# Signs of layer 1's weights copied by VectorE instead of ScalarE, w_out's fold and subtraction moved, and new ranks for the planner

## The chip, the cores and the metric

The kernel runs on one core of a Trainium2 chip. The metric is the device time of one execution in microseconds (us); the lower the better. TensorE (PE) multiplies matrices, VectorE (DVE) and ScalarE (ACT) work elementwise, GpSimd (POOL) also, SyncE (SP) issues most of the DMAs.

## The reference

Attention of 4 batches, 8 heads, 576 positions and 64 channels (four heads with a local mask, four with a strided one), followed by two MLP layers over the 2304 tokens:

```
attn = softmax(mask(q k^T / 8)) v
x = attn as (2304, 512)
h = x @ w_in1;  g = max(0.01 h, h);            x = g @ w_out1      # layer 1, 512 -> 2048 -> 512
h = x @ w_in2;  g = relu(h) + log1p(exp(-|h|)); out = g @ w_out2   # layer 2, softplus
```

The four weights come as 64-bit words, 512 x 2048 or 2048 x 512 of them. Inputs are large enough that the products need more than f16.

## The kernel before, in words

**Products.** A factor is cut into two f16 parts, a high one and the rest, and a product is three matmuls (`mm3`: high by high, high by rest, rest by high; lines 462 to 464). Layer 1 goes by units of 288 tokens (u = 0 to 7): `plan_first` makes the hidden layer, called G0, G1, G2, ... here, `plan_second` the second product, S0, S1, S2, .... Layer 2 goes by 9 units of 256 tokens.

**Weights.** Each weight is prepared in four quarters of 128 x 2048 words. A quarter is loaded by one DMA into an area of the tiles `pair` (`load`); VectorE finds its largest value (`largest`, line 156), from which a power of two for scaling is made (`scale`); it shifts the low words (`low`, line 162). ScalarE scales the high words (`shift`, line 209). Between the two, the sign bit has to get into the low word: for the layer-1 weights W1 (w_in) and O1 (w_out) ScalarE does it behind `shift`, by writing the scaled value as f16 into the upper half of the low word (`sign_of_scaled`, line 205); for the layer-2 weights VectorE does it ahead of `shift`, by copying the sign bit as a 16-bit word (`sign`, line 198). Then VectorE joins the words (`merge`, line 214), ScalarE writes the high f16 part (`high`, line 221), and the rest is a subtraction: for W1 on GpSimd (`rest`, line 226), for O1 on VectorE together with a factor (`rest_of`, line 230). That factor `by` equalizes the scales of W1's quarters; before, `high` and `rest_of` both apply it to O1.

O1's four quarters share one scale (`plan_together`), so none can be scaled before all four are loaded and searched; a quarter of O1 is loaded into the area of W1's quarter of that number once that one has been cut. The high part of an odd quarter of O1 lies where the quarter before it was, and so waits for that one's rest.

**Order.** The program of every engine is written in the order that `Plan.run` finds while the kernel is built. It is a list scheduler: each step has an engine, a cost in us, its dependencies, the PSUM and SBUF places it takes and frees, and a rank. Among the steps that could start on an engine within 0.5 us of the earliest, the one with the lowest rank goes first. A step marked `port` and every step of GpSimd also share one "port" clock. A rank is a pair (start, slope) of the table `RANKS` by the step's name, start + slope x index. Names: L0 to L3 loads of the batches' q, k, v; LW1, LO1, LW2, LO2 loads of weights; A and B the attention's scores and what follows; W1r, W1m, O1r, O1m the steps of a weight before and from its scale; G0, G1, G2, S0, S1, S2 the layer-1 units so named; M later units; F, Fd, Fa, Fp, S layer 2 on PE, DVE, ACT, POOL and PE again. Up to 130 us of its own clock the planner fills longer gaps of PE with matmuls on an identity whose result nobody reads (`idle`, line 92); the profile counts them as busy.

In the schedule before, the attention of batch 0 and the first W1 quarter come first, then G0, G1 and G2 with the attention of batch 1 and the rest of W1 beside them, then O1 and S0, S1, S2, and the later units, with layer 2's weights prepared beside these. S0 takes O1 quarter by quarter; S1 wants all of it.

Of the kernel before, what the change touches and what calls it, by code (L numbers as in the profile page):

```python
# [10 lines left out]
F16 = mybir.dt.float16  # L11
F32 = mybir.dt.float32
# [3 lines left out]
AF = mybir.ActivationFunctionType  # L16
ALU = mybir.AluOpType
# [4 lines left out]
B, H, S, D = 4, 8, 576, 64  # L22
# [15 lines left out]
RING = 5  # L38

RANKS = {  # L40
# [10 lines left out]
}  # L51

F64_LOW = 2.0 ** -11 * 1.625
# [2 lines left out]
def build(tc, qt, kl, ks, v, wi1, wo1, wi2, wo2, mloc, mstr, out):  # L56
    nc = tc.nc
    with ExitStack() as ctx:
# [79 lines left out]
        flat = lambda y: y.rearrange("p a b -> p (a b)")  # L138


        class Weight:
# [57 lines left out]
                    out=w[:, :, :, 1], in0=w[:, :, :, 3], scalar1=0x8000, scalar2=None, op0=ALU.bitwise_and  # L199
                )  # L200

            def sign_of_scaled(self, q):

                w = self.t[q].bitcast(F16).rearrange("p s (n t) -> p s n t", t=4)
                nc.scalar.activation(w[:, :, :, 1], self.words(q)[1].bitcast(F32), AF.Copy)  # L205

            def shift(self, q, s):
                lo, hi = self.words(q)
                nc.scalar.activation(hi.bitcast(F32), hi.bitcast(F32), AF.Copy, scale=s)  # L209
# [7 lines left out]
                )  # L217
                self.f[q] = f.bitcast(F32)

            def high(self, q, hl, by=1.0):  # L220
                nc.scalar.activation(flat(hl[0]), self.f[q], AF.Copy, scale=by)  # L221
                self.hl[q] = hl

            def rest(self, q, eng):
                hi, lo = self.hl[q]
                eng.tensor_tensor(out=flat(lo), in0=self.f[q], in1=flat(hi), op=ALU.subtract)  # L226

            def rest_of(self, q, by):
                hi, lo = self.hl[q]
                nc.vector.scalar_tensor_tensor(  # L230
                    out=flat(lo), in0=self.f[q], scalar=by, in1=flat(hi), op0=ALU.mult, op1=ALU.subtract
                )

            def scale_all(self, g):
                s = self.scale(0, g)
# [351 lines left out]
        W1, O1, W2, O2 = Weight("i1", wi1), Weight("o1", wo1), Weight("i2", wi2), Weight("o2", wo2)  # L587
# [112 lines left out]
        def plan_together(W, name, after, parts, then, w1):  # L700

            st, loads, read, made = {}, [], [], []
            step = lambda eng, cost, fn, deps, k, **kw: plan.add(
                eng, cost, fn, deps, (name + ("r" if k < 3 else "m"), k), **kw
            )
            m = once(lambda: sml.tile([P, 4], F32, name="m4", tag="wm4"))
            for q in range(4):
                ld = plan.add("SP", 5.9, lambda q=q: W.load(q, area(q)), after[q], ("L" + name, q))
                big = step("DVE", 2.2, lambda q=q: W.largest(q, m()[:, q : q + 1]), [ld], q)
                low = step("DVE", 1.14, lambda q=q: W.low(q), [ld], q + 0.1, port=True)  # L710
                loads.append(big)
                read.append([big, low])

            def over():
                st["m"] = sml.tile([P, 1], F32, name="m", tag="wm")
                nc.vector.tensor_reduce(out=st["m"], in_=m(), axis=AX.X, op=ALU.max)

            def all_over():
                st["g"] = to_all(st["m"])

            def scale():
                st["s"] = W.scale_all(largest_of(st["g"]))
                then()

            t = step("DVE", 0.1, over, loads, 3.05)
            t = step("PE", 0.35, all_over, [t], 3.05, take=["pt"])
            t = scaled = step("DVE", 2.3, scale, [t] + w1, 3.06, free=[t])
            for q in range(4):
                y = step("ACT", 2.07, lambda q=q: W.shift(q, st["s"]), [t] + read[q], 4 + q)
                y = step("ACT", 1.9, lambda q=q: W.sign_of_scaled(q), [y], 4 + q)  # L730
                y = step("DVE", 2.2, lambda q=q: W.merge(q), [y], 4 + q, port=True)
                y = step("ACT", 1.85, lambda q=q: W.high(q, parts(q), O1.by[:, q : q + 1]), [y] + made[-1:] * (q % 2), 4 + q)
                made.append(
                    step("DVE", 2.3, lambda q=q: W.rest_of(q, O1.by[:, q : q + 1]), [y], 4 + q, port=True)
                )
            return made, scaled

        def plan_quarter(W, name, q, place, after, parts, after_read, then=None, eng="DVE"):

            st = {}  # L740
            kind = lambda k: name + ("" if then is None else "r" if k < 0.25 else "m")
            step = lambda eng, cost, fn, deps, k, **kw: plan.add(eng, cost, fn, deps, (kind(k), q + k), **kw)

            def big():
                st["m"] = sml.tile([P, 1], F32, name="m", tag="wm")
                W.largest(q, st["m"])

            def over():
                st["g"] = to_all(st["m"])

            def scale():
                st["s"] = W.scale(q, largest_of(st["g"]))
                if then:
                    then(q)

            ld = plan.add("SP", 5.9, lambda: W.load(q, area(place)), after, ("L" + name, q))
            x = step("DVE", 2.2, big, [ld], 0)
            y = step("PE", 0.35, over, [x], 0, take=["pt"])
            sc = step("DVE", 1.45 if then else 1.05, scale, [y], 0.3, free=[y])
            y = step("DVE", 1.14, lambda: W.low(q), [ld], 0.1, port=True)  # L760
            if not then:
                y = step("DVE", 2.35, lambda: W.sign(q), [y], 0.2, port=True)
            y = step("ACT", 2.07, lambda: W.shift(q, st["s"]), [sc, x, y], 0.3)
            if then:
                y = step("ACT", 1.9, lambda: W.sign_of_scaled(q), [y], 0.3)
            y = step("DVE", 2.2, lambda: W.merge(q), [y], 0.4, port=True)
            y = step("ACT", 1.85, lambda: W.high(q, parts(q)), [y] + after_read, 0.5)
            if eng == "Pool":
                return step("Pool", 4.1, lambda: W.rest(q, nc.gpsimd), [y], 0.6), sc
            return step("DVE", 2.3, lambda: W.rest(q, nc.vector), [y], 0.6, port=True), sc  # L770
# [127 lines left out]
        A, A1 = at[0], at[1]  # L898
# [35 lines left out]
        by = lambda n, k=0: lambda i: (n, i + k)  # L934
# [4 lines left out]
        s = {0: plan_second_by_f(0, g[0], o1, by("S0"), a0 + w1_scales)}  # L939
# [26 lines left out]
        for q in range(4):  # L966
            place = (1, 3)[q % 2]
            y, _ = plan_quarter(W2, "W2", q, place, busy[place], in_c, [opened])
# [61 lines left out]
        for q in range(4):  # L1030
            step = lambda eng, cost, fn, deps, k: plan.add(eng, cost, fn, deps, ("O2", q + k), port=eng == "DVE")
            ld = plan.add("SP", 5.9, lambda q=q: O2.load(q, area(1)), busy[1], ("LO2", 4 + q))
            y = step("DVE", 1.14, lambda q=q: O2.low(q), [ld], 0.1)
            y = step("DVE", 2.35, lambda q=q: O2.sign(q), [y], 0.2)
            y = step("ACT", 2.07, lambda q=q: O2.shift(q, late["o2s"]), [y, o2_scaled], 0.3)
            y = step("DVE", 2.2, lambda q=q: O2.merge(q), [y], 0.4)
            sums = step("DVE", 2.5, lambda q=q: o2_sums(q), [y], 0.5)
            y = step("ACT", 1.85, lambda q=q: o2_high(q, "t"), [sums] + (products(7)[4 * q - 4 : 4 * q] if q else busy[3]), 0.6)
            y1 = step("DVE", 2.29, lambda q=q: o2_rest(q, "t"), [y], 0.6)
            y = step("ACT", 1.8, lambda q=q: o2_high(q, "b"), [sums] + ([opened], busy[3], products(7)[12:], [y1])[q] + busy[3], 0.7)  # L1040
# [186 lines left out]
        for u in range(NU2):  # L1227
            U = Unit(u)
            rank = lambda n, k: (n, u * NK + k)
            y = plan.add("DVE", 1.3, U.largest, moved(u), rank("X", 0), behind=highs[-2:-1])  # L1230
            over = plan.add("PE", 0.35, U.over, [y], rank("X", 0), take=["mm"])
            y = plan.add("DVE", 0.75, U.factor, [over], rank("X", 0), free=[over])
# [4 lines left out]
            for k in range(NK):  # L1237
# [11 lines left out]
                y = plan.add("Pool", 1.25, bind(U.add), [soft, relu], rank("Fp", k), free=[size])  # L1249
                y = plan.add("DVE", 0.83, bind(U.sums), [y], rank("Fd", k), port=True)  # L1250
# [4 lines left out]
                y = plan.add("DVE", 1.07, bind(U.cut_rest), [high], rank("Fd", k), free=[relu], port=True)  # L1255
# [84 lines left out]
```

## Time and profile before

| | us |
|---|---|
| median of 3 runs (lowest, highest) | 870.89 (870.03, 873.74) |
| profiled execution, its own time | 871.47 |
| its span, first to last instruction | 869.5 |
| PE busy (fillers included) | 831.9 (96%) |
| PE fillers, line 92 | 21.5, 80 of them |
| DVE busy | 533.7 (61%) |
| ACT busy | 528.3 (61%) |
| POOL busy | 265.0 (30%) |

Busy times are shares of a span in which very different stages follow each other: attention and layer-1 weights in the first 180 us, layer 1 to about 500 us, layer 2 after that. What an engine's work costs has to be read stage by stage, and on PE the fillers have to be taken off. An engine's idle time ahead of an instruction is put down to what released it.

### The profile page before, as it was taken

The numbers are of one execution on the slowest core, as the hardware profiler recorded it, in microseconds if no ns is written. First come the engines' busy times: TensorE is split into PE (matmuls) and PEld (weight loads), VectorE is DVE, ScalarE is ACT, GpSimd is POOL, SyncE is SP. The second block draws the span as 40 slices with busy tenths as digits, with TensorE's granted clock in tenths as the row PEclk, the third lists the DMA queues.
The fourth block names the chain that finished last, engine by engine and source line by source line (L and its number), as shares of the span: only waits on it lengthen the run. The fifth ranks groups of instructions, "written<-read, shape, count | busy, mean of one in ns | idle before, by whom it ended". The sixth has DMA issues, their size and how long they took to land.

```text
span 869.5 us, 17639 instructions
## 1 busy us (share of the span) xinstructions
PE 831.9 (96%) x7330; PEld 684.6 (79%) x7330; DVE 533.7 (61%) x1232; ACT 528.3 (61%) x938; POOL 265.0 (30%) x194
## 2 busy tenths in 40 slices
PE   9888798799999999999999999999999999999997
PEld 5556576578777777787777777888888888888886
DVE  4895652542033535049647859977787778677684
ACT  5899979933456542263726457757575666657572
POOL 2365753120332124140504124323222322223131
PEclk9999999999999999999999999999999999999999
DMA  8932320121013470013221120000000000000000
GB/s 329 390 126 112 140 98 1 67 81 56 1 58 138 158 304 25 2 41 154 98 97 29 71 98 1 26 2 25 2 25 2 25 2 26 1 26 1 26 25 25
DMA packets 10991, 63.27 MB, mean 73 GB/s; under 512 B 1344, under 2 KB 1440, under 8 KB 7840
## 3 DMA queue, kind: packets, MB, share of 16 engines
q1 hardware_dynamic: 10656, 62.00, 19.0%
q8 instruction: 57, 0.93, 0.4%
q10 hardware_dynamic: 256, 0.16, 0.1%
q14 instruction: 22, 0.18, 0.1%
HBM read 57.44 MB, written 4.72 MB: 71 GB/s over the span
## 4 chain that ended last, share of the span: by engine, by line
PE 69%; ACT 12%; DVE 11%; DMA 3%; issue 3%; POOL 1%; SPq 0%; DVEq 0%; ACTq 0%; POOLq 0%
PE h L462 11%; PE h L464 11%; PE h L463 11%; PE o L462 10%; PE o L464 10%; PE o L463 10%; ACT pair L205 3%; ACT pair L209 2%; DMA pair<-wo_dram 2%; ACT s L368 2%; PE ps L322 2%; DVE pair L1005 2%; PE po L419 2%; PE pt L399 1%; ACT t L483 1%
## 5 line engine op out<-in xcount | busy, mean ns | idle before, releaser
L462 PE MATMUL h<-x,w 128*128 128x256 f16 (+1 forms) x1088 | 303.5, 279 | 7.2 <-ACT t L483 5.0
L464 PE MATMUL h<-x,w 128*128 128x256 f16 (+1 forms) x1088 | 303.4, 279 | 4.3 <-POOL w L226 4.3
L463 PE MATMUL h<-x,w 128*128 128x256 f16 (+1 forms) x1088 | 303.4, 279 | 0.0
L1155 POOL TENSOR_TENSOR pair<-pair,t 128x512 f32<-128x512 f32 x72 | 100.4, 1394 | 268.6 <-ACT t L1151 171.1
L489 POOL TENSOR_TENSOR g<-t,g 128x576 f16<-128x576 f32 x64 | 104.3, 1633 | 183.7 <-ACT g L486 181.7
L462 PE MATMUL o<-g,pair 128*128 128x288 f16 x512 | 147.7, 288 | 2.8 <-ACT pair L221 1.8
L464 PE MATMUL o<-g,pair 128*128 128x288 f16 x512 | 147.6, 288 | 2.5 <-DVE pair L230 2.5
L463 PE MATMUL o<-g,pair 128*128 128x288 f16 x512 | 147.5, 288 | 0.0
L463 PEld LDWEIGHTS <-w 128*128 128x128 f16 x1088 | 106.5, 98 | 27.3 <-issue 8.7
L464 PEld LDWEIGHTS <-w 128*128 128x128 f16 x1088 | 106.4, 98 | 24.3 <-POOL w L226 5.2
L462 PEld LDWEIGHTS <-w 128*128 128x128 f16 x1088 | 106.4, 98 | 19.4 <-issue 0.2
L1167 ACT ACTIVATE gr<-pair,x2b 128x896 f16<-128x896 f32 x72 | 74.0, 1038 | 57.2 <-DVE pair L1163 57.2
L1171 DVE SCALAR_TENSOR_TENSOR gr<-pair,x2b,gr 128x896 f16<-128x896 f32 x72 | 86.4, 1209 | 24.8 <-ACT gr L1167 24.7
L1163 DVE TENSOR_TENSOR pair<-pair 128x128 f32<-128x128 f32 x288 | 80.2, 324 | 16.8 <-POOL pair L1155 14.3
L1143 ACT ACTIVATE pair<-h,x2s 128x512 f32<-128x512 f32 x72 | 49.0, 680 | 60.0 <-DVE t L1136 54.4
L464 PE MATMUL o<-w,gr 128*128 128x256 f16 x306 | 83.4, 273 | 0.9 <-DVE gr L1171 0.7
L462 PE MATMUL o<-w,gr 128*128 128x256 f16 x306 | 83.4, 273 | 0.0
L463 PE MATMUL o<-w,gr 128*128 128x256 f16 x306 | 83.4, 273 | 0.0
L390 POOL TENSOR_TENSOR s<-s,sm 96x512 f32<-96x512 f32 (+3 forms) x48 | 43.7, 931 | 121.4 <-DVE sm L385 64.1
L483 ACT ACTIVATE t<-h,gs 128x576 f32<-128x576 f32 x64 | 47.0, 735 | 49.0 <-PE h L464 48.8
L1136 DVE TENSOR_SCALAR t<-h 128x512 int32<-128x512 int32 x72 | 48.7, 685 | 29.0 <-PE h L464 28.4
L214 DVE SCALAR_TENSOR_TENSOR pair<-pair 128x2048 int32<-128x2048 int32 x16 | 37.4, 2338 | 45.9 <-ACT pair L205 35.3
(123 smaller groups left out, 1391.1 us busy)
## 6 DMA issues: line engine op xcount, KB each, us to landing
pair<-wo_dram SPq DMA_DIRECT2D x12, 2048.0 KB, 7.8
pair<-wi_dram SPq DMA_DIRECT2D x8, 2048.0 KB, 10.1
out_dram<-pair SPq DMA_DIRECT2D x18, 256.0 KB, 2.2
q<-qt_dram SPq DMA_DIRECT2D x12, 288.0 KB, 5.9
v<-v_dram SPq DMA_DIRECT2D x2, 1408.0 KB, 7.7
pair<-v_dram SPq DMA_DIRECT2D x2, 1408.0 KB, 6.0
k<-ks_dram SPq DMA_DIRECT2D x7, 288.0 KB, 3.3
k<-kl_dram SPq DMA_DIRECT2D x5, 304.0 KB, 3.8
```

What stands on the lines that cost most here:

```text
L390: nc.gpsimd.tensor_tensor(out=sv, in0=sv, in1=rs, op=ALU.mult)
L462: nc.tensor.matmul(ps, ah, bh, start=first, stop=False)
L463: nc.tensor.matmul(ps, ah, bl, start=False, stop=False)
L464: nc.tensor.matmul(ps, al, bh, start=False, stop=last)
L483: nc.scalar.activation(t, ps, AF.Prelu, scale=gates[f // 4], alpha=0.01)
L489: nc.gpsimd.tensor_tensor(out=g[:, 1, f : f + 2, :], in0=t, in1=g[:, 0, f : f + 2, :], op=ALU.subtract)
L1136: nc.vector.tensor_scalar(out=t.bitcast(I32), in0=self.ps[k].bitcast(I32), scalar1=0x7FFFFFFF, scalar2=None, op0=ALU.bitwise_and)
L1143: nc.scalar.activation(r[:, :4].rearrange("p (j h) n -> p j (h n)", j=2), self.ps[k], AF.Relu, scale=self.sc[:, k // 2 : k // 2 + 1],)
L1155: nc.gpsimd.tensor_tensor(out=r, in0=r, in1=self.a[k], op=ALU.add)
L1163: nc.vector.tensor_tensor(out=r[:, o], in0=r[:, x], in1=r[:, y], op=op)
L1167: nc.scalar.activation(self.a[k][:, 0], self.r[k][:, 1:], AF.Copy, scale=self.ag)
L1171: nc.vector.scalar_tensor_tensor(out=a[:, 1], in0=self.r[k][:, 1:], scalar=self.ag, in1=a[:, 0], op0=ALU.mult, op1=ALU.subtract)
```

## The change

W1 and O1 now get their signs as the layer-2 weights do, by `sign` on VectorE between `low` and `shift`; `sign_of_scaled` goes. For O1 the factor `by` is applied by a step of its own, `fold`, on ScalarE ahead of `high`, and the rest is the plain subtraction on GpSimd. The planner's ranks are all new.

```diff
@@ -38,16 +38,16 @@
 RING = 5
 
 RANKS = {
-    "A0": (904.756, 0.733), "A1": (1181.967, 5.007), "A2": (1400.517, 32.745), "A3": (-265.753, 0.202),
-    "B0": (380.721, 6.480), "B1": (387.831, 20.804), "B2": (1471.672, 0.086), "B3": (530.207, 2.562),
-    "E": (291.606, 0.206), "F": (-267.727, 13.512), "Fa": (61.151, 23.937), "Fd": (809.007, 5.868),
-    "Fp": (-127.497, 0.075), "G0": (-198.498, 0.175), "G1": (1158.664, 0.271), "G2": (688.143, 68.364),
-    "L0": (132.415, 11.820), "L1": (916.455, 23.686), "L2": (379.055, 0.154), "L3": (438.906, 5.033),
-    "LO1": (1218.018, 120.000), "LO2": (32.727, 1.176), "LW1": (1078.973, 8.302), "LW2": (1265.162, 4.586),
-    "M": (448.423, 4.303), "O1m": (1374.727, 1.358), "O1r": (1361.947, 3.960), "O2": (1374.878, 3.426),
-    "O2l": (1380.929, 1.863), "S": (1139.158, 120.000), "S0": (1133.607, 120.000), "S1": (1442.075, 3.830),
-    "S2": (1500.000, 39.240), "W1m": (975.007, 5.818), "W1r": (1347.663, 2.158), "W2": (753.358, 37.166),
-    "X": (491.589, 120.000),
+    "A0": (593.918, 6.350), "A1": (1468.724, 0.341), "A2": (1303.427, 4.470), "A3": (216.970, 32.247),
+    "B0": (459.638, 0.221), "B1": (567.439, 1.007), "B2": (1330.328, 3.772), "B3": (576.954, 0.139),
+    "E": (173.808, 1.720), "F": (898.565, 106.393), "Fa": (569.105, 19.350), "Fd": (1148.152, 42.979),
+    "Fp": (-297.956, 5.862), "G0": (54.794, 0.688), "G1": (1312.962, 16.894), "G2": (147.860, 96.965),
+    "L0": (223.674, 0.318), "L1": (999.347, 78.176), "L2": (306.754, 120.000), "L3": (138.752, 6.844),
+    "LO1": (1241.476, 106.640), "LO2": (429.009, 3.186), "LW1": (902.225, 10.533), "LW2": (465.142, 0.058),
+    "M": (469.071, 4.299), "O1m": (1097.393, 0.092), "O1r": (573.462, 83.106), "O2": (1343.153, 26.107),
+    "O2l": (938.674, 0.191), "S": (1283.540, 120.000), "S0": (372.637, 29.244), "S1": (835.251, 88.854),
+    "S2": (1238.551, 120.000), "W1m": (1336.966, 41.822), "W1r": (1392.864, 35.415), "W2": (790.250, 41.348),
+    "X": (677.612, 120.000),
 }
 
 F64_LOW = 2.0 ** -11 * 1.625
@@ -199,11 +199,6 @@
                     out=w[:, :, :, 1], in0=w[:, :, :, 3], scalar1=0x8000, scalar2=None, op0=ALU.bitwise_and
                 )
 
-            def sign_of_scaled(self, q):
-
-                w = self.t[q].bitcast(F16).rearrange("p s (n t) -> p s n t", t=4)
-                nc.scalar.activation(w[:, :, :, 1], self.words(q)[1].bitcast(F32), AF.Copy)
-
             def shift(self, q, s):
                 lo, hi = self.words(q)
                 nc.scalar.activation(hi.bitcast(F32), hi.bitcast(F32), AF.Copy, scale=s)
@@ -217,19 +212,16 @@
                 )
                 self.f[q] = f.bitcast(F32)
 
-            def high(self, q, hl, by=1.0):
-                nc.scalar.activation(flat(hl[0]), self.f[q], AF.Copy, scale=by)
+            def fold(self, q, by):
+                nc.scalar.activation(self.f[q], self.f[q], AF.Copy, scale=by)
+
+            def high(self, q, hl):
+                nc.scalar.activation(flat(hl[0]), self.f[q], AF.Copy)
                 self.hl[q] = hl
 
             def rest(self, q, eng):
                 hi, lo = self.hl[q]
                 eng.tensor_tensor(out=flat(lo), in0=self.f[q], in1=flat(hi), op=ALU.subtract)
-
-            def rest_of(self, q, by):
-                hi, lo = self.hl[q]
-                nc.vector.scalar_tensor_tensor(
-                    out=flat(lo), in0=self.f[q], scalar=by, in1=flat(hi), op0=ALU.mult, op1=ALU.subtract
-                )
 
             def scale_all(self, g):
                 s = self.scale(0, g)
@@ -708,8 +700,9 @@
                 ld = plan.add("SP", 5.9, lambda q=q: W.load(q, area(q)), after[q], ("L" + name, q))
                 big = step("DVE", 2.2, lambda q=q: W.largest(q, m()[:, q : q + 1]), [ld], q)
                 low = step("DVE", 1.14, lambda q=q: W.low(q), [ld], q + 0.1, port=True)
+                sign = step("DVE", 2.35, lambda q=q: W.sign(q), [low], q + 0.2 + 0.86 * (q == 3), port=True)
                 loads.append(big)
-                read.append([big, low])
+                read.append([big, sign])
 
             def over():
                 st["m"] = sml.tile([P, 1], F32, name="m", tag="wm")
@@ -727,12 +720,10 @@
             t = scaled = step("DVE", 2.3, scale, [t] + w1, 3.06, free=[t])
             for q in range(4):
                 y = step("ACT", 2.07, lambda q=q: W.shift(q, st["s"]), [t] + read[q], 4 + q)
-                y = step("ACT", 1.9, lambda q=q: W.sign_of_scaled(q), [y], 4 + q)
                 y = step("DVE", 2.2, lambda q=q: W.merge(q), [y], 4 + q, port=True)
-                y = step("ACT", 1.85, lambda q=q: W.high(q, parts(q), O1.by[:, q : q + 1]), [y] + made[-1:] * (q % 2), 4 + q)
-                made.append(
-                    step("DVE", 2.3, lambda q=q: W.rest_of(q, O1.by[:, q : q + 1]), [y], 4 + q, port=True)
-                )
+                y = step("ACT", 1.8, lambda q=q: W.fold(q, O1.by[:, q : q + 1]), [y], 4 + q)
+                y = step("ACT", 1.85, lambda q=q: W.high(q, parts(q)), [y] + made[-1:] * (q % 2), 4 + q)
+                made.append(step("Pool", 4.1, lambda q=q: W.rest(q, nc.gpsimd), [y], 4 + q))
             return made, scaled
 
         def plan_quarter(W, name, q, place, after, parts, after_read, then=None, eng="DVE"):
@@ -758,11 +749,8 @@
             y = step("PE", 0.35, over, [x], 0, take=["pt"])
             sc = step("DVE", 1.45 if then else 1.05, scale, [y], 0.3, free=[y])
             y = step("DVE", 1.14, lambda: W.low(q), [ld], 0.1, port=True)
-            if not then:
-                y = step("DVE", 2.35, lambda: W.sign(q), [y], 0.2, port=True)
+            y = step("DVE", 2.35, lambda: W.sign(q), [y], 0.2, port=True)
             y = step("ACT", 2.07, lambda: W.shift(q, st["s"]), [sc, x, y], 0.3)
-            if then:
-                y = step("ACT", 1.9, lambda: W.sign_of_scaled(q), [y], 0.3)
             y = step("DVE", 2.2, lambda: W.merge(q), [y], 0.4, port=True)
             y = step("ACT", 1.85, lambda: W.high(q, parts(q)), [y] + after_read, 0.5)
             if eng == "Pool":
```

## Rows read from the trace of the kernel before

**Rows 1.** Windows: stretch, length; busy us (instructions) of PE, PEld, DVE, ACT, POOL; clock; DMA.

```profile
0.00:51.30 51.30, 44.79 (x366) 26.81 (x367) 35.56 (x95) 36.43 (x131) 13.81 (x19) 1.00 0.79 312
51.30:126.00 74.70, 63.32 (x575) 48.94 (x574) 47.58 (x126) 67.15 (x133) 51.34 (x31) 1.00 0.37 134
126.00:187.00 61.00, 52.62 (x415) 40.07 (x412) 30.76 (x65) 52.11 (x63) 18.13 (x13) 0.94 0.15 53
...
500.00:550.00 50.00, 46.05 (x410) 39.57 (x409) 40.52 (x60) 31.59 (x41) 17.00 (x9) 1.00 0.12 43
550.00:862.00 312.00, 312.00 (x2860) 279.70 (x2858) 232.51 (x547) 194.07 (x269) 83.38 (x64) 1.00 0.04 15
```

**Rows 2.** The same stretches, PE's filler matmuls alone.

```profile
0.00:51.30 51.30, 20.39 (x77) 1.00 0.79 312
51.30:126.00 74.70, 1.15 (x3) 1.00 0.37 134
```

**Rows 3.** Groups by line on ScalarE: busy us, mean ns, then idle before and releaser.

```profile
L205 ACT ACTIVATE pair<-pair 128x2048 f16<-128x2048 f32 x8 | 38.3, 4784 | 0.1
...
L209 ACT ACTIVATE pair<-pair,s 128x2048 f32<-128x2048 f32 x12 | 26.4, 2200 | 8.6 <-DVE s L188 8.5
...
L221 ACT ACTIVATE pair<-pair,by_o 128x2048 f16<-128x2048 f32 x4 | 8.0, 1992 | 0.0
```

**Rows 4.** Groups by line on VectorE, then GpSimd.

```profile
L214 DVE SCALAR_TENSOR_TENSOR pair<-pair 128x2048 int32<-128x2048 int32 x16 | 37.4, 2338 | 45.9 <-ACT pair L205 35.3 <-ACT pair L209 10.6
...
L162 DVE TENSOR_SCALAR pair<-pair 128x2048 uint32<-128x2048 uint32 x16 | 23.1, 1457 | 12.0 <-DMA pair<-wo_dram 12.0
L198 DVE TENSOR_SCALAR pair<-pair 128x2048 uint16<-128x2048 uint16 x8 | 20.7, 2592 | 0.2
...
L230 DVE SCALAR_TENSOR_TENSOR pair<-pair,by_o 128x2048 f16<-128x2048 f32 x4 | 9.4, 2348 | 6.2 <-ACT pair L221 6.2
...
L226 POOL TENSOR_TENSOR w<-pair,w 128x2048 f16<-128x2048 f32 x4 | 16.3, 4084 | 13.1 <-ACT w L221 13.1
```

**Rows 5.** Windows: the stretch in which ScalarE prepares W1 and O1, and a slow-clock one.

```profile
37.00:178.00 141.00, 118.76 (x1008) 88.72 (x1008) 86.08 (x227) 130.72 (x218) 67.13 (x42) 0.98 0.28 103
171.00:177.00 6.00, 4.38 (x19) 2.78 (x20) 6.00 (x3) 6.00 (x24) 0.00 (x0) 0.50 0.00 0
```

**Rows 6.** Timeline, start and length in us: W1's first quarter and batch 0's end.

```profile
39.88 4.77 ACT L205 ACTIVATE pair<-pair 128x2048 f16<-128x2048 f32 x1
44.38 0.63 ACT L407 ACTIVATE a<-pt 108x432 f32<-108x432 f32 x1
...
49.09 4.08 POOL L226 TENSOR_TENSOR w<-pair,w 128x2048 f16<-128x2048 f32 x1 [10.13 <-ACT w L221]
...
53.35 0.41 DVE L458 TENSOR_TENSOR x<-po,x 128x108 f16<-128x108 f32 x2
```

**Rows 7.** Timeline of SyncE's queue: the load of W1's first quarter.

```profile
15.66 0.43 SPq L147 DMA_DIRECT2D pair<-wi_dram  x1
```

**Rows 8.** Waits of PE, 51.3 to 126 us: total, times, longest.

```profile
PE h L464 <- POOL w L226: 4.3, 3, 2.2
PE pt L399 <- ACT a L407: 3.0, 3, 1.7
PE po L419 <- ACT a L407: 2.2, 1, 2.2
```

**Rows 9.** Waits of PE, 126 to 187 us.

```profile
PE h L462 <- ACT t L483: 3.1, 3, 1.9
PE o L464 <- DVE pair L230: 2.5, 1, 2.5
```

**Rows 10.** Timeline of VectorE and GpSimd at 520 us, and the latter's group.

```profile
520.00 2.47 DVE L198 TENSOR_SCALAR pair<-pair 128x2048 uint16<-128x2048 uint16 x1
...
520.01 3.44 POOL L1155 TENSOR_TENSOR pair<-pair,t 128x512 f32<-128x512 f32 x1 [1.99 <-ACT pair L1143]
...
L1155 POOL TENSOR_TENSOR pair<-pair,t 128x512 f32<-128x512 f32 x72 | 100.4, 1394 | 268.6 <-ACT t L1151 171.1 <-ACT pair L1143 93.9 <-DVE pair L1202 3.5
```

## The prediction

> **What bounds the kernel now.** I read the page's engine table first: PE is busy for 96% of the span, so a gain can only come from time in which PE does nothing useful. Its fillers are counted as busy, so I took windows by stage and subtracted them. To 51.3 us, where the first layer-1 product starts, PE is idle 51.3 - 44.79 = 6.51 us and runs 20.39 us of fillers: 26.9 us without use [rows 1, 2]. From there to 126 us it is idle 11.38 us and runs 1.15 us of fillers: 12.5 us [rows 1, 2]. From 126 to 187 us (the end of S0) it is idle 8.38 us [rows 1], and from 171 to 177 us the granted clock was 0.50, that is 1.2 GHz, after the waits for O1; 4.38 us of matmuls there would have taken half at 2.4 GHz, so 2.2 us more [rows 5]: 10.6 us. Layer 2 stands otherwise: 550 to 862 us is all busy, and 500 to 550 us lacks 3.95 us [rows 1]. So 50 us without use lie in the first 187, and what a change to W1 and O1 is worth is decided there.
>
> Next, who is late there. The waits of PE name ScalarE, directly (the copies of transposed scores, L407, and the bend, L483) or one step back, where GpSimd's subtraction L226 or VectorE's L230 waited for ScalarE's `high` [rows 8, 9]. From 37 to 178 us ScalarE is busy 130.7 of 141 us, 93% [rows 5]: it is the engine that sets the pace of the front. And its costliest weight step there is the one that the change removes: `sign_of_scaled` takes 4784 ns, eight times, 38.3 us [rows 3], where the code before gives the planner 1.9 us. The order before was thus laid out for a ScalarE with 8 x 2.88 = 23 us less to do than it has.
>
> **The change part by part.**
>
> *Signs off ScalarE.* 8 x 4.784 = 38.3 us go [rows 3]. Of this 4 x 4.784 lie in W1 and as much in O1.
>
> *Fold on ScalarE.* Four activations of 128x2048, f32 to f32 in place with a scale from a column. No row is the same; the nearest are `shift`, f32 in place by a column, at 2.20 us, and `high` with a column on the same contiguous source, at 1.99 us [rows 3]. I take 2.0 us, 8 us in all; the bounds are 1.9 (`high` without its column operand can't cost more than with it) and, if an in-place write behaves as in L205, 4.78 us [rows 3]. ScalarE's balance is -38.3 + 8.0 = -30.3 us, at the upper bound -19.2. `high` loses its column; I cost that at nothing.
>
> The Trainium skill, "ScalarE: Activation LUTs", section "What ACT_TABLE_LOAD costs", states one element per cycle and lane for any function, about 186 ns + 0.833 ns per element, which is an estimated 1.9 us for L205. By that page the removed steps would be worth 15 us and the balance -7 us, and the change would be nearly idle. The trace agrees for L221 (1.99 us) and not for L205 (4.78 us) [rows 3]; the measurement decides.
>
> *Signs on VectorE.* Eight `sign` at 2.592 us mean (the layer-2 weights have the same step now), 20.7 us; minus four `rest_of` at 2.348, 9.4 us: +11.3 us [rows 4]. VectorE is busy 86.1 of 141 us there [rows 5], so it has room. `shift` now also waits for `sign`; behind a waiting `shift` in ScalarE's queue stand fetches, exponentials and bends, and PE waits for those. `low` and `sign` need only the load, so this wait is late only where the load is, that is in W1's first quarter.
>
> *Rest of O1 on GpSimd.* 4 x 4.084 = 16.3 us [rows 4], for 2.348 on VectorE: 1.74 us more from `high` to the last part, and an odd quarter's `high` waits for the rest before it. GpSimd is busy 67.1 of 141 us [rows 5]; what queues behind such a subtraction there are the spreads of attention and the cuts of g. SyncE's loads of later v's wait for O1's rests too, at most those 1.74 us later.
>
> *The shared port.* At 520.00 us a `sign` of 2.47 us starts, and GpSimd's L1155, issued 0.01 us later, takes 3.44 us, while its mean is 1.394 [rows 10]: the two don't run side by side. The Trainium skill, "SBUF — State Buffer", section "SBUF: two separate sides", calls it an exclusive lock: of GpSimd and certain VectorE instructions the first holds the shared ports to its end. The trace agrees with that, by the same rows. So `sign` and O1's subtraction add 20.7 + 16.3 - 9.4 = 27.6 us to what VectorE and GpSimd must do one after the other. This is a rival below.
>
> *Ranks.* They add no work. Three things are read from the table. W1's loads (LW1 902 to 934) now come ahead of batch 1's (L1 999), where before they came behind them (1079 against 916); the first was issued at 15.66 us [rows 7] and can now go out earlier, so that `low` and `sign` can run while batch 0's attention still holds PE. S0 (372, slope 29, was 1134, slope 120) now goes ahead of G1 (1313) and of the later part of G2 (148, slope 97): when a quarter of O1 is late, PE has G1 or G2 to do. And layer 2's F has slope 106 for 13.5, which moves products that are all covered now.
>
> *The sum.* First stretch: W1's first quarter loses the 4.77 us of L205 and gains at worst one `sign` in front of `shift`, 2.47 (rows 10's): 2.3 to 4.8 us. Batch 0's end moves with it, since its fetch at 44.38 us stood right behind that L205, and x was ready at 53.35, when GpSimd's cut of the quarter had just ended at 53.17 [rows 6]. I take 3.4 us; from 0 (batch 0 keeps its time) to 8 (the early load). Second stretch: 12.5 us, of which fetches make 5.2 and W1's cuts 4.3 [rows 8]; three L205 (14.4 us) leave a ScalarE that was busy 67.2 of 74.7 us [rows 1], so PE, with 62.2 us of useful work, becomes the longer one. I leave 5.5 and take 7.0; from 2 to 11. Third stretch: ScalarE's part of a quarter of O1 falls from 2.2 + 4.8 + 2.0 = 9.0 to 2.2 + 2.0 + 2.0 = 6.2 us [rows 3], and the whole starts earlier. Of 10.6 us (bends 3.1, L230 2.5 [rows 9], the clock 2.2, other waits) I leave 4.1 and take 6.5; from 2 to 10. Later stretches: nothing, they are covered by PE. Sum 16.9: 871.47 - 16.9 = 854.6 for the profiled execution's time (its span plus 2.0). The median shown is 0.6 lower, so 854.0.
>
> **The rivals.**
>
> *The port becomes the pace.* From 37 to 178 us GpSimd holds 67.1 us [rows 5] and VectorE's L214, L162 and L230 8 x 2.338 + 8 x 1.457 + 4 x 2.348 = 39.7 us [rows 4]: 106.8 of 141, 76% (an upper bound, since recorded lengths hold waits). With 27.6 more it is 134.4; W1's four `low` and `sign`, 16.2 us, may go ahead of 37 us, which leaves 118. My second and third stretch want this in 141 - 13.5 = 127.5 us, 93%. If no better than 87% can be packed, it takes 136 and 5 us remain of the 13.5; with 3.4 of the first stretch the gain is 8.4 less the longer subtraction 1.7, about 7: 864. For it: rows 10. Against: the planner counts a port itself.
>
> *PE alone is the pace.* All is hidden, and W1's early load makes G0 start sooner: 8 + 11 + 8 = 27 less some latency of the last cut, 26: 845. Against: fetches and transposes of batch 1 still alternate between PE and ScalarE.
>
> *Slower, from layer 2.* The place is the softplus stage, where VectorE was busy 40.5 of 50 us at 500 us and PE lost 3.95 us, while at 75% of VectorE (232.5 of 312) it lost none [rows 1]. If the new ranks, by F's slope above all, order that stage so that PE waits for VectorE's pieces throughout, at that rate, 312 / 50 x 3.95 = 24.6 us come back: 879. It decides from 17 us on. Against: VectorE's work there is unchanged and has 25% of air.
>
> *The order eats it.* The signs are cheaper, but new ranks put them in front of softmax's short steps, and PE waits for these as long as it did for ScalarE: 870.
>
> **How the numbers follow.** Forecast 0.60 (854); port 0.18 (864); PE alone 0.11 (845); order 0.05 (870); layer 2 0.06 (879). A measurement of this kernel tells 0.5%, 4.35 us, from no change. Faster by more (below 866.5): the first three but for 0.01, 0.88; within: 0.06; slower: 0.06. The range: the forecast's own bounds reach from gains of 4 to 29, the likely part 846 to 862; taken to the neighbours' cases 843 to 867.
>
> **What would show it.** No L205-like activation of 4.8 us on ScalarE; `fold` at about 2.0 us; `sign` sixteen times at 2.5 to 2.7 instead of eight; ScalarE under 85% busy over the stretch from the first `shift` to O1's last `high`; the first layer-1 product by 48 to 50 us; S0's end 13 to 22 us earlier; no slow clock within S0; 550 us to the end unchanged in length. Wrong: a fold near 4.8 us; PE's waits for L226 grown past 10 us (the port); idle PE after S0, or more than 5 us of it in the softplus stage.

## The result, and the profile after

The changed kernel takes 861.48 us (861.21 to 861.51, 3 runs) against 870.89: a ratio of 0.9872, 95% interval 0.9848 to 0.9895. That is 9.4 us less, where 16.9 were forecast. The profiled span falls from 869.5 to 859.7 us.

From the page: busy time of each engine (share of the span, instructions), and the shares of the chain of work that ended last.

```profile
PE 834.1 (97%) x7353; PEld 686.2 (80%) x7353; DVE 552.7 (64%) x1236; ACT 499.7 (58%) x934; POOL 289.4 (34%) x198
...
PE 63%; DVE 18%; ACT 7%; DMA 5%; issue 4%; POOL 3%; DVEq 0%; POOLq 0%; ACTq 0%
```

PE's busy time says nothing here, it holds 103 fillers instead of 80. ScalarE does 28.6 us less than before, VectorE 19 and GpSimd 24 us more. In the chain VectorE has risen from 11% to 18% and ScalarE fallen from 12% to 7%.

Windows of the changed kernel: stretch, length, busy us (instructions) of PE, PEld, DVE, ACT and POOL, granted clock, DMA share, GB/s.

```profile
0.00:44.60 44.60, 40.89 (x327) 23.63 (x327) 31.59 (x67) 28.37 (x111) 14.66 (x18) 1.00 0.86 351
44.60:60.00 15.40, 9.71 (x61) 6.89 (x62) 13.33 (x21) 7.07 (x8) 8.71 (x3) 0.78 0.38 137
60.00:130.00 70.00, 65.65 (x601) 49.24 (x600) 62.55 (x172) 53.22 (x156) 47.46 (x29) 1.00 0.33 117
130.00:200.00 70.00, 68.71 (x585) 54.46 (x583) 32.55 (x79) 46.77 (x76) 37.11 (x19) 1.00 0.18 63
37.00:178.00 141.00, 129.42 (x1105) 97.08 (x1103) 105.49 (x238) 104.70 (x218) 91.90 (x49) 0.98 0.29 104
51.00:55.00 4.00, 4.00 (x19) 2.49 (x18) 4.00 (x3) 1.91 (x1) 0.00 (x0) 0.50 0.88 279
60.00:80.00 20.00, 19.93 (x178) 15.48 (x177) 19.39 (x37) 12.87 (x37) 14.57 (x9) 1.00 0.33 120
```

The same, PE's fillers alone: busy (count), clock, DMA share, GB/s.

```profile
0.00:44.60 44.60, 20.54 (x73) 1.00 0.86 351
...
60.00:130.00 70.00, 8.15 (x30) 1.00 0.33 117
```

Against [rows 1, 2, 5] one sees: before the first layer-1 product PE is idle 3.7 us and runs 20.5 us of fillers (24.3, was 26.9); just behind it 5.7 us are idle and 4 us run at a clock of 0.50, 1.2 GHz, which costs 2.0 (7.7 in all, was part of the next stretch); from 60 to 130 us it is 4.35 + 8.15 = 12.5; and from 130 to 200 us, where S0 now is, only 1.3 us are idle at full clock (was 10.6 for the like work). ScalarE from 37 to 178 us is at 74%, was 93%.

Groups of the changed kernel (busy us, mean ns of one, idle before and its releaser): the fold, the sign, GpSimd's subtractions for W1 and for O1.

```profile
L216 ACT ACTIVATE pair<-pair,by_o 128x2048 f32<-128x2048 f32 x4 | 8.0, 1990 | 0.0
...
L198 DVE TENSOR_SCALAR pair<-pair 128x2048 uint16<-128x2048 uint16 x16 | 43.8, 2735 | 0.3
...
L224 POOL TENSOR_TENSOR w<-pair,w 128x2048 f16<-128x2048 f32 x4 | 18.2, 4559 | 6.4 <-ACT w L219 6.4
L224 POOL TENSOR_TENSOR pair<-pair 128x2048 f16<-128x2048 f32 x4 | 17.2, 4295 | 4.6 <-ACT pair L219 4.6
```

The fold costs 1.99 us (2.0 taken). `sign` has a mean of 2.74 us over sixteen (2.59 before [rows 4]), GpSimd's subtractions 4.56 and 4.30 us (4.08 before [rows 4]): all of them are longer for waiting on one another.

### The profile page after: what moved, and what is told of

Read it like the earlier page. It is cut to its first block, busy times and chain, and to the rows that moved or that the text cites. A ratio compares the mean times of both kernels' runs of the same rounds, so it can differ in the third digit from the quotient of the medians.

```text
span 859.7 us, 17683 instructions
## 1 busy us (share of the span) xinstructions
PE 834.1 (97%) x7353; PEld 686.2 (80%) x7353; DVE 552.7 (64%) x1236; ACT 499.7 (58%) x934; POOL 289.4 (34%) x198
## 4 chain that ended last, share of the span: by engine, by line
PE 63%; DVE 18%; ACT 7%; DMA 5%; issue 4%; POOL 3%; DVEq 0%; POOLq 0%; ACTq 0%
PE h L454 10%; PE h L456 10%; PE h L455 10%; PE o L454 10%; PE o L456 10%; PE o L455 10%; DMA pair<-wo_dram 3%; DVE pair L198 3%; DVE gr L1159 2%; ACT pair L204 2%; PE ps L314 2%; DVE pair L162 2%; POOL w L224 2%; DVE pair L209 2%; DVE m L156 1%
## 5 line engine op out<-in xcount | busy, mean ns | idle before, releaser
L1159 DVE SCALAR_TENSOR_TENSOR gr<-pair,x2b,gr 128x896 f16<-128x896 f32 x72 | 86.4, 1211 | 27.4 <-ACT gr L1155 26.9
L1151 DVE TENSOR_TENSOR pair<-pair 128x128 f32<-128x128 f32 x288 | 78.3, 316 | 20.2 <-POOL pair L1143 17.7
L382 POOL TENSOR_TENSOR s<-s,sm 96x512 f32<-96x512 f32 (+3 forms) x48 | 49.7, 1055 | 113.4 <-DVE sm L377 72.5
L456 PEld LDWEIGHTS <-pair 128*128 128x128 f16 x512 | 50.0, 98 | 13.8 <-POOL pair L224 1.2
```

Source lines behind the costliest of these rows:

```text
L382: nc.gpsimd.tensor_tensor(out=sv, in0=sv, in1=rs, op=ALU.mult)
L456: nc.tensor.matmul(ps, al, bh, start=False, stop=last)
L1151: nc.vector.tensor_tensor(out=r[:, o], in0=r[:, x], in1=r[:, y], op=op)
L1159: nc.vector.scalar_tensor_tensor(out=a[:, 1], in0=self.r[k][:, 1:], scalar=self.ag, in1=a[:, 0], op0=ALU.mult, op1=ALU.subtract)
```

## The experiments

Of all runs the reference point is the kernel before on the same chip; its median there was 872 to 873 us. Ratios are to it, with a 95% interval. The changed kernel's own is 0.9872 [0.9848, 0.9895]. Four runs first put steps and order apart.

**New steps under the old ranks.**

```diff
 (the changed kernel)
-RANKS = { ... new ... }
+RANKS = { ... those of the kernel before ... }
```

> The changed steps (signs by VectorE, fold, O1's rest on GpSimd) under the ranks of before. Theory 'ScalarE's load': the 30 us less of ScalarE work carry the gain whatever the order, so most of the 9.4 us stays: 862 to 866. Rival 'the ranks': without the new order nothing is gained: 869 to 873.

916.63 us, 1.0511 [1.0485, 1.0537]. Neither.

**Old steps under the new ranks.**

```diff
 (the kernel before)
-RANKS = { ... old ... }
+RANKS = { ... those of the changed kernel ... }
```

> The steps of before (signs by ScalarE, 4.78 us each) under the new ranks. Theory 'ScalarE's load': ScalarE still has 38 us of signs in the front, so 868 to 878. Rival 'the ranks': the early loads of W1 and S0 ahead of G1 carry the gain: 860 to 864.

917.11 us, 1.0514 [1.0489, 1.0539]. Neither.

**The kernel before, the planner told the true cost of its sign.**

```diff
-y = step("ACT", 1.9, lambda q=q: W.sign_of_scaled(q), [y], 4 + q)
+y = step("ACT", 4.78, lambda q=q: W.sign_of_scaled(q), [y], 4 + q)
...
-    y = step("ACT", 1.9, lambda: W.sign_of_scaled(q), [y], 0.3)
+    y = step("ACT", 4.78, lambda: W.sign_of_scaled(q), [y], 0.3)
```

> The kernel before, with one number changed: the planner is told 4.78 us for the sign step on ScalarE instead of 1.9; ranks and steps as before. Theory 'ScalarE's load': the work is the same and ScalarE is the pace, 867 to 872. Rival 'the plan was misled': an order laid out for the true cost hides most of it, 860 to 865.

915.15 us, 1.0491 [1.0466, 1.0516]. One cost put right, and 44 us are lost. None of the three came out at either number expected for it. In all three most of the loss lies between 100 and 200 us. Windows of the first, new steps under the old ranks (columns as above):

```profile
100.00:150.00 50.00, 31.23 (x237) 23.42 (x235) 34.65 (x51) 22.94 (x56) 26.65 (x17) 0.80 0.22 85
150.00:200.00 50.00, 28.13 (x226) 22.50 (x225) 19.09 (x55) 40.40 (x62) 29.23 (x13) 0.73 0.14 49
```

PE is busy 59 of 100 us and the clock falls to 0.80 and 0.73. So each of these two tables fits one set of costs and steps; under the three other pairings tried the order starves PE, and the kernel took some 44 us longer. Swapping tables can't tell what the steps are worth. From here on the order is held: the planner plans as it did, and only what a step issues is changed.

**Signs by VectorE in the order of before.**

```diff
 (the kernel before; planned as before, issued elsewhere)
-step("ACT", 1.9, lambda q=q: W.sign_of_scaled(q), ...)
+step("ACT", 1.9, lambda q=q: W.sign(q), ...)
...
-step("ACT", 1.9, lambda: W.sign_of_scaled(q), ...)
+step("ACT", 1.9, lambda: W.sign(q), ...)
```

> The kernel before with its order of every engine kept as it was planned, and only the eight sign steps of layer 1 issued on VectorE (2.5 us) in the place where ScalarE had them (4.78 us). Nothing else changes: no fold, no GpSimd, no new ranks. Theory 'ScalarE sets the pace, and a foreign order is what cost 45 us': with the order kept, taking 38 us off ScalarE gains what the change gained or more, 855 to 864. Rival 'the gain is the new order's alone': 868 to 873.

864.51 us, 0.9917 [0.9887, 0.9947]; its profiled span is 861.3 us, 8.2 under the kernel before. Its window, columns as above:

```profile
37.00:178.00 141.00, 126.36 (x1072) 95.23 (x1070) 111.87 (x243) 98.52 (x213) 82.03 (x48) 0.98 0.31 118
```

ScalarE is busy 98.5 of 141 us, was 130.7 [rows 5]; PE 126.4, was 118.8. One step moved, without fold, GpSimd or new ranks, gives 7 to 8 of the 9.4 us. What fold, GpSimd and ranks add, some 2 us, no run splits, and the two intervals overlap. Where the gain lies, in the stretches of [rows 1] and with the fillers of the first of them:

```profile
51.30:126.00 74.70, 65.11 (x573) 49.85 (x573) 59.09 (x128) 54.60 (x131) 57.45 (x31) 0.98 0.36 134
126.00:187.00 61.00, 58.55 (x478) 45.93 (x475) 45.41 (x83) 36.32 (x62) 20.57 (x13) 0.97 0.15 53
...
51.30:126.00 74.70, 1.40 (x3) 0.98 0.36 134
```

From 126 to 187 us PE is idle 2.45 us, was 8.38; from 51.3 to 126 it is idle 9.59 and runs 1.40 of fillers, 11.0, was 12.5. So already in the old order the stretch of O1 gains and that of W1's later quarters hardly does.

**Signs back on ScalarE in the new order.**

```diff
 (the changed kernel; planned as it is)
-step("DVE", 2.35, lambda q=q: W.sign(q), ...)
+step("DVE", 2.35, lambda: None, ...)
...
-lambda q=q: W.shift(q, st["s"])
+lambda q=q: (W.shift(q, st["s"]), W.sign_of_scaled(q))
 (W1 likewise)
```

> The changed kernel with its planned order kept, and the eight signs of layer 1 issued on ScalarE behind shift, 4.78 us each, instead of on VectorE; fold and GpSimd's rest stay. Theory 'ScalarE sets the pace': ScalarE gets 38 us back in an order that has no room for them in 100 to 165 us, 872 to 890. Rival 'the new order': it has slack on ScalarE (102 of 130 us busy), so 860 to 866.

893.23 us, 1.0242 [1.0219, 1.0265]. The waits of PE (line and operand, waited for; total us, times, longest):

```profile
PE h L459 <- ACT t L480: 13.7, 6, 4.4
PE pt L396 <- ACT a L404: 9.7, 3, 5.2
PE o L461 <- POOL pair L229: 5.8, 3, 4.1
```

The time is above both ranges. The waits name ScalarE's bends and fetches, and the cuts behind its `high`. The new order has no room for 38 us on ScalarE.

**W1's first subtraction on VectorE.**

```diff
-return step("Pool", 4.1, lambda: W.rest(q, nc.gpsimd), [y], 0.6), sc
+return step("Pool", 4.1, lambda: W.rest(q, nc.gpsimd if q else nc.vector), [y], 0.6), sc
```

> The changed kernel with the subtraction of W1's first quarter issued on VectorE instead of GpSimd, at the same place of the order. Theory 'port and clock': in the changed kernel this subtraction took 5.99 us because a sign on VectorE held the port, PE waited 5.64 us for it and then ran 6.8 us at 1.2 GHz. On VectorE, behind the sign, it takes 2.3 us: PE waits about 4.3 us, or less, and the clock may stay; 857 to 860. Rival 'VectorE is the pace of 40 to 90 us': the 2.3 us more on VectorE delay the next quarters, and PE's wait comes back as fillers at 80 to 96 us: 861 to 863.

863.24 us, 0.9897 [0.9882, 0.9912]. PE's wait fell from 5.6 to 4.3 us, and the time didn't: the rival's number.

**The second quarter's sign on ScalarE**, which frees the port for that first subtraction.

```diff
-lambda: W.sign(q)
+lambda: None if then and q == 1 else W.sign(q)
...
-lambda: W.shift(q, st["s"])
+lambda: (W.shift(q, st["s"]), then and q == 1 and W.sign_of_scaled(q))
```

> The changed kernel with its order kept, and the sign of W1's second quarter alone issued on ScalarE. Theory 'port and clock': GpSimd's first subtraction is no longer held (4.1 instead of 5.99 us), PE waits 3.8 instead of 5.64 us, and the clock falls later or not at all: 857 to 860. Rival 'VectorE is late anyway': the second quarter's merge is no earlier and PE loses it again before 100 us: 860.5 to 862.5.

862.51 us, 0.9889 [0.9862, 0.9916]: no gain that can be measured. A wait of PE and GpSimd's first subtraction there:

```profile
PE h L461 <- POOL w L229: 4.8, 2, 3.7
...
43.88 4.09 POOL L229 TENSOR_TENSOR w<-pair,w 128x2048 f16<-128x2048 f32 x1 [5.77 <-ACT w L224]
```

The subtraction took 4.09 instead of 5.99 us, and the longest wait fell from 5.6 to 3.7 us as expected; the span moved by 1.0 us (858.7), which the spread of the runs (860.49 to 864.81) covers. So the collision is there, and what it costs is too little to be measured here; the sign on ScalarE may have taken back a part.

**No fillers after the first quarter.**

```diff
-self.idle(n, y)
+if clock["PE"] < 55.0:
+    self.idle(n, y)
```

> The changed kernel with its order kept, and the 30 filler matmuls of 60 to 95 us left out (they compute nothing). Theory 'they stand in a wait': PE waits for VectorE's and ScalarE's part of the later W1 quarters there, so without them it idles instead, and the time stays 860.5 to 863, with the clock falling at worst. Rival 'they are the loss': 30 x 0.215 = 6.5 us of the lost gain are the fillers themselves, 855 to 858.

864.14 us, 0.9905 [0.9878, 0.9933], so not faster, and 1 us above the first range. The window of 60 to 100 us:

```profile
60.00:100.00 40.00, 35.65 (x301) 27.57 (x299) 35.73 (x115) 31.75 (x103) 29.93 (x16) 0.83 0.28 97
```

The mean clock there falls to 0.83 (1.00 with the fillers). The fillers stand in a wait and hold the clock; they are not what the time was lost to.

**O1's signs later on VectorE.**

```diff
-sign = step("DVE", 2.35, lambda q=q: W.sign(q), ...)
+sign = step("DVE", 2.35, lambda: None, ...)
...
-lambda q=q: W.merge(q)
+lambda q=q: (W.sign(q), W.merge(q))
```

> The changed kernel with its planned order kept; only the four signs of O1 are issued on VectorE right ahead of O1's merges (133 to 155 us, where VectorE is one third busy) instead of behind O1's low (66 to 126 us). Theory 'VectorE's queue is the pace of 60 to 113 us' (O1's largest, low and sign stand ahead of W1's third and fourth quarter there, and the chain that ended last runs through them): two to three signs of 2.5 us go from ahead of W1's last quarters, 857 to 860 by its time, W1's third subtraction ends 3 to 5 us earlier. Rival 'S0 then waits for O1': each quarter's way gets 2.5 us longer and PE gives it back there, 861 to 864.

870.00 us, 0.9961 [0.9948, 0.9974]. Waits of PE, and GpSimd's subtraction of W1's third quarter:

```profile
PE o L456 <- POOL pair L224: 7.1, 3, 4.2
PE h L456 <- POOL w L224: 6.6, 2, 5.6
...
92.42 4.08 POOL L224 TENSOR_TENSOR w<-pair,w 128x2048 f16<-128x2048 f32 x1
...
77.53 2.48 DVE L198 TENSOR_SCALAR pair<-pair 128x2048 uint16<-128x2048 uint16 x1
...
80.31 0.29 DVE L127 TENSOR_REDUCE g<-pm 128x1 f32<-128x128 f32 x1 [0.30 <-PE pm L122]
```

PE waits 7.1 us for O1's subtractions, the rival's way, and the third quarter's ended at 96.50 us as before (96.36), though a sign of O1 no longer stood ahead of it at 67.3 and at 73.8 us. The time is above both ranges. So the work of O1's signs on VectorE is not what makes the third quarter late. VectorE's order is not excluded by this: the quarter's own sign, still behind batch 1's attention there, began at 77.53 us (78.25 in the changed kernel).

**O1's low and signs later.**

```diff
 (as o1_sign_late, and)
-lambda q=q: W.low(q)
+lambda: None
...
-lambda q=q: (W.sign(q), W.merge(q))
+lambda q=q: (W.low(q), W.sign(q), W.merge(q))
```

> As o1_sign_late, and O1's four low steps also issued right ahead of the merges. Theory 'port': the low of 107.9 us, which took 5.00 us because GpSimd's subtraction of W1's last quarter held the port, is no longer on the way; PE's wait of 2.1 us at 113.6 us goes: 855 to 859. Rival: VectorE then needs 6 us in a row for each O1 quarter, as long as PE works on one, and S0 waits: 861 to 866.

875.63 us, 1.0030 [1.0013, 1.0046]. PE's wait for O1's subtractions is 10.2 us. The low of 107.9 us went and with it PE's wait of 2.1 us, as expected; the wait for O1 took back more, and the time is above both ranges.

**The removed step by itself.**

```diff
+nc.scalar.activation(half(t), hi(t), AF.Copy)
+nc.scalar.activation(half(u), hi(t), AF.Copy)
+nc.scalar.activation(flat16, hi(t), AF.Copy)
+nc.scalar.activation(half(u), row, AF.Copy)
+nc.scalar.activation(lo(t), hi(t), AF.Copy)
+nc.scalar.activation(half(t), lo(t), AF.Copy)
```

> The changed kernel with twelve activations on ScalarE added behind its end, on weights no longer needed (2 x 6 forms of 128x2048, time of the whole means nothing here): the half-word write in place from the high word of the same 64 bits (the removed step's form), the same into another tile, a contiguous f16 write from the strided source, a half-word write into another tile from a contiguous source, a full-word write in place of the low word, a half-word write in place from the low word itself. Theory 'half-word writes at 8-byte stride are slow': forms 1, 2, 4 and 6 take 4.8 us, forms 3 and 5 about 2.0. Rival 'the overlap of source and target is slow': forms 1, 5 and 6 take 4.8 us, forms 2, 3 and 4 about 2.0.

The first of the two rounds, start and length in us:

```profile
854.55 4.74 ACT L1264 ACTIVATE pair<-pair 128x2048 f16<-128x2048 f32 x1
859.02 4.79 ACT L1265 ACTIVATE pair<-pair 128x2048 f16<-128x2048 f32 x1
863.85 2.01 ACT L1266 ACTIVATE pair<-pair 128x2048 f16<-128x2048 f32 x1
865.89 4.74 ACT L1267 ACTIVATE pair<-pair 128x2048 f16<-128x2048 f32 x1
870.66 2.00 ACT L1268 ACTIVATE pair<-pair 128x2048 f32<-128x2048 f32 x1
872.69 4.73 ACT L1269 ACTIVATE pair<-pair 128x2048 f16<-128x2048 f32 x1
```

4.7 to 4.8 us for the four that write half-words at a stride of 8 bytes, 2.0 us for the contiguous f16 and for the full word at the same stride. Overlap plays no part.

**O1's subtractions, and W1's last, on VectorE with an order of their own.**

```diff
-made.append(step("Pool", 4.1, lambda q=q: W.rest(q, nc.gpsimd), [y], 4 + q))
+made.append(step("DVE", 2.3, lambda q=q: W.rest(q, nc.vector), [y], 4 + q, port=True))
...
-in_a, [], gate_scale, "Pool") for q in range(4)]
+in_a, [], gate_scale, "Pool" if q < 3 else "DVE") for q in range(4)]
-RANKS = { ... of the changed kernel ... }
+RANKS = { ... searched with the planner's own costs ... }
```

> The changed kernel with signs by VectorE and the fold kept, but the subtractions of all four O1 quarters and of W1's last one on VectorE (2.3 us) instead of GpSimd (4.1 to 6 us), and ranks searched anew for these steps. Theory 'signs are the gain; GpSimd's subtractions only hold the port': with an order made for it the kernel is at least as fast as the changed one, 855 to 860, GpSimd's busy time falls by 20 us, and no low or merge takes over 4 us in the front. Rival 'GpSimd's part of the change is needed': VectorE, with 11.5 us more, becomes late and PE waits for it, 863 to 875.

878.06 us, 1.0056 [1.0036, 1.0076]: a miss. Windows, columns as above:

```profile
60.00:100.00 40.00, 31.07 (x273) 23.60 (x271) 36.40 (x118) 29.62 (x96) 29.55 (x17) 0.92 0.34 122
100.00:200.00 100.00, 99.41 (x881) 79.03 (x880) 62.84 (x131) 71.42 (x134) 37.41 (x25) 1.00 0.21 74
200.00:450.00 250.00, 243.82 (x2106) 193.62 (x2105) 99.63 (x256) 112.30 (x252) 65.33 (x52) 0.99 0.24 87
450.00:550.00 100.00, 91.74 (x767) 75.18 (x766) 71.45 (x94) 53.82 (x65) 28.09 (x16) 0.98 0.18 64
```

From 100 to 200 us PE loses 0.6 us, so in this order O1 doesn't need GpSimd there. GpSimd's busy time fell by 23 us and no low or merge took over 2.6 us, as expected. What PE lacks is elsewhere: 8.9 us in 60 to 100 (1.8 in the changed kernel, fillers counted as busy), and 14.4 us from 200 to 550 (4.5). Steps and ranks were changed together here, so whether the new order or the steps are late is not shown; the time is above both ranges. No run was measurably faster than the changed kernel.

## Why the prediction was right, and where it was off

*ScalarE's signs were the pace.* Shown, by two runs with held order: taking them off gains 7 to 8 us in the old order, putting them back costs 32 us in the new. The fold's price was right to 0.01 us, and the sign's was confirmed by itself (4.73 to 4.79 us). That it is a matter of the half-word write and not of the data's overlap was shown by the probe. What the prediction cites from the Trainium skill's page "ScalarE: Activation LUTs", section "What ACT_TABLE_LOAD costs", would have made the change nearly idle; the trace's 4.78 us was the one to go by.

*First stretch, 3.4 us: mis-sized.* The first product came 6.6 us sooner (51.27 to 44.64 us), W1's load being early. But it needs the subtraction too, and that came only 2.5 us sooner. In the changed kernel, start and length:

```profile
44.39 2.44 DVE L198 TENSOR_SCALAR pair<-pair 128x2048 uint16<-128x2048 uint16 x1
...
44.66 5.99 POOL L224 TENSOR_TENSOR w<-pair,w 128x2048 f16<-128x2048 f32 x1 [5.77 <-ACT w L219]
...
44.64 0.30 PE L454 MATMUL h<-x,w 128*128 128x288 f16 x1 [0.77 <-ACT w L219]
...
50.70 0.42 PE L456 MATMUL h<-x,w 128*128 128x288 f16 x1 [5.64 <-POOL w L224]
```

VectorE's sign of the next quarter held the port when GpSimd wanted it, the subtraction took 5.99 us, PE stood 5.64 us and then ran at 1.2 GHz. The stream of products thus restarted 2.5 us sooner than it had begun before (53.22 to 50.70 us), less the 2.0 us of the slow clock: about 0.5 of the 3.4 us. I had counted the way from `high` to the product as unchanged, with one `sign` ahead of `shift` as its only new cost. (The expectation of `first_rest_dve` says 6.8 us at 1.2 GHz; PE ran about 4 of them, and was idle before.)

*Second stretch, 7.0 us: this term failed.* I left 5.5 of 12.5 us, and 12.5 are there, though ScalarE has room. Its busy share from 60 to 130 us is 53 of 70. What is late is W1's third quarter, in the changed kernel:

```profile
52.72 2.27 DVE L156 TENSOR_REDUCE m<-pair 128x1 f32<-128x2048 f32 x1
54.91 1.21 DVE L162 TENSOR_SCALAR pair<-pair 128x2048 uint32<-128x2048 uint32 x1
...
67.34 2.50 DVE L198 TENSOR_SCALAR pair<-pair 128x2048 uint16<-128x2048 uint16 x1
...
73.80 2.50 DVE L198 TENSOR_SCALAR pair<-pair 128x2048 uint16<-128x2048 uint16 x1
...
78.25 2.61 DVE L198 TENSOR_SCALAR pair<-pair 128x2048 uint16<-128x2048 uint16 x1
...
79.93 0.38 PE L122 MATMUL pm<-ident,m 128*128 128x128 f32 x2
...
83.09 2.17 ACT L204 ACTIVATE pair<-pair,s 128x2048 f32<-128x2048 f32 x1
...
92.29 4.07 POOL L224 TENSOR_TENSOR w<-pair,w 128x2048 f16<-128x2048 f32 x1
```

Its largest value is known at 54.99 us and its `low` ends at 56.12. Then three engines are late with it together. VectorE gives it its own `sign` only at 78.25 us, to 80.86 (the signs at 67.34 and 73.80 are O1's: they went when O1's signs were moved). PE issues the small matmul that spreads the largest value over the partitions at 79.93, when the products with two quarters have run out, and VectorE reads its result without an idle moment behind that sign:

```profile
80.67 0.25 DVE L127 TENSOR_REDUCE g<-pm 128x1 f32<-128x128 f32 x1
```

ScalarE begins `shift` at 83.09 (75.69 in the kernel before), and the parts are ready at 96.36. In between PE has batch 1's attention and fillers. So by this trace an earlier matmul alone would move nothing, since sign and `shift` stand late as well. The step of the prediction that failed is that `shift` waits for `sign` only in W1's first quarter, because `low` and `sign` need only the load: in the third, `sign` came 22 us behind `low`, by the order of VectorE. In the old order with the signs moved the third quarter came no sooner either (its subtraction began at 89.60 us, 89.21 before). The runs exclude the fillers and the work of O1's signs as causes. Whether an order with all three steps early would bring the 7 us was not tried and stays open.

*Third stretch, 6.5 us: under-sized.* 10.6 us fell to 1.3, that is 9.3: no slow clock, no wait for O1 over 0.3 us. By count of its 192 products S0 ended about 10.5 us sooner, at 176 us, where 13 to 22 were forecast. That S0 comes ahead of G1's and G2's rest is read from the ranks, but they are not needed for most of this: in the old order with the signs moved the like idle time fell from 8.4 to 2.5 us and S0 ended about 7.4 us sooner.

The three terms thus came out near 0.5, 0 and 9.3 for 3.4, 7.0 and 6.5. That the time still fell into the range is in part luck: the third gave 2.8 us more than forecast where the first two gave 9.9 less. Their sum equals the 9.8 us that the span lost, but the first is counted by the start of the products and the others by idle time. As an account of PE this is rough. Idle time, fillers and slow clock of the front, added up as in the prediction, fall only from 50.0 to 45.8 us (24.3 + 7.7 + 12.5 + 1.3). But a filler is recorded at 0.28 us on average while in a run of them one follows the other every 0.22 us, so recorded time overstates what they take, and the changed kernel has 23 more. By spacing (103 and 80 times 0.22) the front falls by about 6.3 us and the stretch from 187 to 500 us of before by 1.5; some 2 us stay unplaced.

*The rivals.* The port's number (864) was nearer than mine (854), its mechanism was not: the collisions happen, a second one being this, start and length in the changed kernel,

```profile
107.88 5.00 DVE L162 TENSOR_SCALAR pair<-pair 128x2048 uint32<-128x2048 uint32 x1
...
107.71 4.09 POOL L224 TENSOR_TENSOR w<-pair,w 128x2048 f16<-128x2048 f32 x1 [0.62 <-ACT w L219]
```

where `low` takes 5.00 instead of 1.22 us as GpSimd's subtraction runs, but freeing the first gave no gain that could be measured, and taking the second off the way was outweighed by the wait for O1. In these rows, of the two, the later one waits for the end of the other. That is the lock that the Trainium skill, "SBUF — State Buffer", section "SBUF: two separate sides", states for GpSimd and certain VectorE instructions, and the trace agrees. "PE alone is the pace" nearly holds from 113 to 450 us (1.9 of 337 us idle), not before. "Slower, from layer 2" did not come: from 450 to 550 us 4.5 us are idle (4.2 before), and 550 to 849 us lack 0.2.

## What to carry to other kernels

When an engine is relieved, look in the order of the other engines for what will be late next, and check every step of the chain: here the gain came where O1 is prepared, in either order, and was nil where one quarter's sign, small matmul and `shift` all stood late in their queues. To learn what a step is worth under a planner, hold the order and change what is issued; a plan made anew for one altered cost moved this kernel by 44 us. A mean load over 141 us ("VectorE has room") hides a stretch in which it is full: 19.4 of 20 us from 60 to 80 us.

## What the runs showed of the hardware

An activation on ScalarE that writes 16-bit values 8 bytes apart takes 4.7 to 4.8 us for 128x2048, the same with 32-bit values 2.0 us. A 16-bit `tensor_scalar` on VectorE with that stride, at 2.4 to 2.5 us by itself, holds up a subtraction on GpSimd that is issued while it runs: 5.99 us for 4.09.
